# Decode block with adaptive layer norm: K/V rows of 24576 bytes in tiles of four heads, and a ring of four slots that also holds other weights

## The chip, the cores and the metric

The kernel runs on one core of a Trainium2 chip. The metric is the device time of one execution in microseconds (us): the median of several runs. A profile of one execution shows when each engine worked. TensorE (PE) does matrix products, VectorE (DVE) and ScalarE (ACT) work on tiles in SBUF and PSUM, GpSimd (POOL) fills constants, and SyncE (SP) issues nearly all transfers from HBM. SBUF has 128 partitions.

## The reference

One token per batch (B = 2) passes through attention over a cached window and a gated feed-forward network, both with a layer norm that is scaled and shifted by a condition `c`:

```python
mod = (silu(c) @ w_mod).reshape(2, 6, 1, 640)        # sa, ca, ga, sb, cb, gb
h = layernorm(x) * (1 + ca) + sa
q = (h @ wq)                                         # 32 heads of 192
k, v = last 1024 positions of the caches             # of 4096, per batch and head
o = softmax(q @ k.T * 192**-0.5) @ v
x = x + ga * (o.reshape(2, 1, 6144) @ wo)
h = layernorm(x) * (1 + cb) + sb
x = x + gb * ((gelu(h @ w_gate) * (h @ w_up)) @ w_down)
```

D is 640, F is 1536, all inputs are bf16. The two caches give 25.2 MB each (2 batches x 32 heads x 1024 keys x 192), w_mod 4.9 MB, wq and wo 7.9 MB each, and the three FFN weights 5.9 MB: 76.9 MB in all.

## The kernel before, in words

The program is a list of operations for each engine, written out by a small scheduler (`_Sched`, lines 28 to 101): `S.op` and `S.dma` append to an engine's list in the order of the Python code, and note which operations must have ended (reads and writes of named keys). Each engine runs its list in order; an operation that waits holds back all that stands behind it on that engine. Transfers from SP are one such list.

**Loads.** SP issues w_mod (38400 B per partition, line 297, into tile `r3`), then wq (61440 B per partition, line 298, into `r1`), and then the tiles of K and V into a ring of `NS` = 6 slots (`declare_ring`, lines 316 to 329). Afterwards it issues wo, into the memory of wq (lines 562 to 567), and w_gate, w_up and w_down in six pieces, into the memory of w_mod (568 to 582). These stand behind the last tile of V in SP's list.

**Tiles of K and V.** A tile holds two heads of both batches: 128 partitions are 32 groups `q` x 2 heads x 2 batches (`HB` = 4), and a partition has `J` = 32 keys of 192 numbers, 12288 B in a row of HBM. There are `NG` = 16 tiles of each kind. One transfer loads one batch's 64 partitions, so a tile is two transfers. The order is k0, k1, then k(g) and v(g-2) in turn. A slot is loaded again when the tile in it has been used.

**q.** `q_unit` (399 to 416) multiplies `hbm`, a tile that holds h spread over partitions, with a part of wq, so that each partition gets the q of its own head and batch: 10 matmuls of 384 columns for two tiles, then a copy to `qbc` by ScalarE. Two units run before the loop, and `filler` (418 to 429) runs the others inside the loop. Once they are all done, a filler is four matmuls of 512 columns whose result isn't used.

**The loop** (529 to 559) goes over tiles g, with later steps of the tiles before interleaved:

- `d_mul(g)`: VectorE multiplies the K tile by q (line 436).
- `p_reduce(g, part)`: TensorE adds up products over chunks of 16 numbers with an identity matrix, 12 matmuls of 512 columns (line 449); after the second half the K slot is free.
- `d_rows`, `p_maxT`, `d_max`: row sums, the partition maximum, a transpose, and the maximum of each head (458 to 473).
- `p_bias`, `d_bias`: two small matmuls spread the maximum and a large negative number for the partitions of other heads; VectorE adds it, ScalarE takes the exponent into `E_sb` with a column for every head and batch of the tile (476 to 489).
- `p_pv(g)`: TensorE multiplies E with V, 16 matmuls, four at a time in quarters of the array (line 499); then the V slot is free and ScalarE copies the result (506).
- `p_sel`, `d_norm`, `d_oT`: selection by constant matrices `SEL` and `DS`, division by the sum, and a transpose into `oT`, for two tiles together (509 to 527).

Steps of a tile stretch over four iterations. After the loop, five groups of matmuls multiply `oT` with wo (584 to 592), and the rest follows in order: `x1`, `layer_norm` (339 to 365), `ffn_gu` for gate and up, gelu, product, down, and the output by two transfers, one on SP and one on ScalarE's queue (636 and 637).

Ahead of the loop: POOL and VectorE build constants, `c` and `x` come by two transfers each on ScalarE's queue (lines 252 to 254), and `mod_part(0)`, the first layer norm and `mod_part(1)` follow when w_mod has landed.

Of the kernel before, what the change touches and what calls it, by code (L numbers as in the profile page):

```python
# [103 lines left out]
def bass_adaLN_cond__sliding_block_cached__geglu_ffn__decode_kernel(  # L104
# [23 lines left out]
    assert B == 2 and Dh == 192 and H % 4 == 0  # L128
# [6 lines left out]
    HB = 4  # L135
    QP = P // HB
    J = W // QP
    NQ = H * Dh
    NT = NQ // P
    NG = H // 2  # L140
    NGG = NG // 2
    ST = 4 * Dh // P
    SCALE = float(Dh) ** -0.5
    EPS = 1e-5
    GC = 512 // J
# [5 lines left out]
    NS = 6  # L151
    WO_SPLIT = [2, 2, 2, 1, 1]
    NWO = len(WO_SPLIT)
    assert sum(WO_SPLIT) == NGG
# [5 lines left out]
    QUP = 2  # L160
# [3 lines left out]
    with es:  # L164
# [6 lines left out]
        R3N = max(KT * 6 * D + KT * 2 * P, 2 * KT * F + FT * D)  # L171
        r3 = sb("r3", [P, R3N], BF16)
        wm_v = r3[:, 0:KT * 6 * D].rearrange("p (k n) -> p k n", k=KT)
        hbm_v = r3[:, KT * 6 * D:KT * 6 * D + KT * 2 * P].rearrange("p (k e m) -> p k e m", k=KT, e=2)
        wg_v = r3[:, 0:KT * F].rearrange("p (k n) -> p k n", k=KT)
        wu_v = r3[:, KT * F:2 * KT * F].rearrange("p (k n) -> p k n", k=KT)
        wd_v = r3[:, 2 * KT * F:2 * KT * F + FT * D].rearrange("p (f n) -> p f n", f=FT)
        qbc = sb("qbc", [P, NG, Dh], BF16)
        ring = sb("ring", [P, NS, J, Dh], BF16)
# [4 lines left out]
        P4 = sb("P4", [P, HB], F32)  # L184
        Bsel = sb("Bsel", [P, P], F32)
        SEL = sb("SEL", [P, 2, 2, P], BF16)
        DS = sb("DS", [P, 2, P], F32)
        par8 = sb("par8", [HB, P], F32)
        noff = sb("noff", [HB, HB], F32)
        zero_f = sb("zero_f", [HB, HB], F32)  # L190
# [15 lines left out]
        gmn = sb("gmn", [1, 2, HB], F32)  # L206
# [4 lines left out]
        rden = sb("rden", [P, 1], F32)  # L211
        oc = sb("oc", [P, Dh], BF16)
# [27 lines left out]
        sem_out = [S.sem("d_out%d" % i) for i in range(2)]  # L240
# [5 lines left out]
        def rows_of(tile, b):  # L246
            return tile[b:b + SQ * (NJ - 1) + 1:SQ, :]

        S.op("pool", lambda e: e.memset(cc[:, :], 0.0), writes=[("cc", 0), ("cc", 1)], name="cc0")
        S.op("pool", lambda e: e.memset(xc[:, :], 0.0), writes=[("xc", 0), ("xc", 1)], name="xc0")  # L250
        for b in range(2):
            S.dma("act", k_dma(rows_of(cc, b), c[b, :].rearrange("(j n) -> j n", j=NJ)), sem_c, writes=[("cc", b)], name="ld_c%d" % b)
        for b in range(2):
            S.dma("act", k_dma(rows_of(xc, b), A_x[b, 0, :].rearrange("(j n) -> j n", j=NJ)), sem_x, writes=[("xc", b)], name="ld_x%d" % b)
# [8 lines left out]
        S.op("pool", lambda e: e.affine_select(out=par8[:, :].rearrange("k (q c) -> k q c", c=HB),  # L263
                                               in_=ones_f[0:HB, :].rearrange("k (q c) -> k q c", c=HB),
                                               pattern=[[0, QP], [-1, HB]], compare_op=ALU.is_equal, fill=0.0,
                                               base=0, channel_multiplier=1),
             reads=["ones_f"], writes=["par8"], name="par8")
        S.op("pool", lambda e: e.affine_select(out=noff[:, :], in_=zero_f[:, :], pattern=[[-1, HB]],
                                               compare_op=ALU.is_equal, fill=BIG, base=0, channel_multiplier=1),
             reads=["zero_f"], writes=["noff"], name="noff")  # L270
        S.op("pool", lambda e: e.memset(SEL[:, :, :, :], 0.0), writes=["SEL"], name="SEL0")
        S.op("pool", lambda e: e.memset(DS[:, :, :], 1.0), writes=["DS"], name="DS1")
        hb0 = S.op("pool", lambda e: e.memset(hbm_v, 0.0), writes=["hbm"], name="hbm0")
# [3 lines left out]
        S.op("dve", lambda e: e.tensor_reduce(out=P4[:, :], in_=ident_f[:, :].rearrange("p (q c) -> p c q", c=HB), axis=AX.X, op=ALU.add),  # L277
             reads=["ident_f"], writes=["P4"], name="P4")
# [3 lines left out]

        for z in range(2):
            for jj in range(2):
                S.op("dve", (lambda z, jj: lambda e: e.tensor_copy(
                    out=SEL[:, z, jj, :].rearrange("p (a m) -> p a m", m=SQ)[:, 2 * z:2 * z + 2, 0:2],
                    in_=G32[:, HB * jj:HB * jj + HB].rearrange("p (h b) -> p h b", b=2)))(z, jj),
                    reads=["G32"], writes=["SEL"], name="SEL%d%d" % (z, jj))
            S.op("dve", (lambda z: lambda e: e.memset(DS[:, z, :].rearrange("p (a m) -> p a m", m=SQ)[:, :, 0:2], 0.0))(z),
                 writes=["DS"], name="DS0%d" % z)  # L290
            S.op("dve", (lambda z: lambda e: e.tensor_copy(
                out=DS[:, z, :].rearrange("p (a m) -> p a m", m=SQ)[:, 2 * z:2 * z + 2, 0:2],
                in_=P4[:, :].rearrange("p (h b) -> p h b", b=2)))(z),
                reads=["P4"], writes=["DS"], name="DS%d" % z)

        keep = {}
        keep["wm_dma"] = S.dma("sp", k_dma(r3[:, 0:KT * 6 * D], w_mod.rearrange("(p k) n -> p (k n)", k=KT)), sem_wm, writes=["wm"], name="ld_wm")
# [4 lines left out]
        for g in range(NG + 2):  # L302
            if g < NG:
                items.append(("k", g))
            if g >= 2:
                items.append(("v", g - 2))
# [6 lines left out]
        def ring_keys(slot):  # L313
            return [("ring", slot, b) for b in range(2)]

        def declare_ring(*consumed):
            ring_state["done"].update(place[it] for it in consumed)
            while ring_state["next"] < len(items) and (ring_state["next"] < NS or (ring_state["next"] - NS) in ring_state["done"]):
                s = ring_state["next"]
                kind, g = items[s]  # L320
                slot = s % NS
                cache = A_v_cache if kind == "v" else A_k_cache
                for b in range(2):
                    S.dma("sp", k_dma(ring[b:P:2, slot, :, :].rearrange("p j d -> p (j d)"),
                                      cache[b, 2 * g:2 * g + 2, K0:Sk, :].rearrange("h (q j) d -> q h (j d)", q=QP)),
                          sem_ring[slot], writes=[("ring", slot, b)], name="ld_%s%d_%d" % (kind, g, b))
                ring_state["next"] += 1

        declare_ring()


# [3 lines left out]
        S.op("act", lambda e: e.activation(out=sc[:, :], in_=cc[:, :], func=ACTF.Silu), reads=[("cc", 0), ("cc", 1)], writes=["sc"], name="silu")  # L335
        to_contraction(scT[:, :, :], sc[:, :], KT, ["sc"], ["scT"], "scT")
        S.op("dve", lambda e: e.tensor_copy(out=X2[:, 0, :], in_=xc[:, :]), reads=[("xc", 0), ("xc", 1)], writes=[("X2", 0)], name="x_f32")
# [30 lines left out]
        mod_pe = []  # L368

        def mod_part(part):  # L370
# [10 lines left out]
            mod_pe.append(S.op("pe", f, reads=["scT", "wm"], writes=[bank(bk)], name="mod%d" % part))  # L381
# [9 lines left out]
        for h in range(2):  # L391
            S.op("dve", (lambda h: lambda e: e.tensor_copy(
                out=hbm_v[:, :, h, :].rearrange("p k (q e b) -> p k q e b", e=2, b=2)[:, :, :, h, :],
                in_=hT[:, :, 0:2].unsqueeze(2).broadcast_to([P, KT, QP, 2])))(h),
                reads=["hT"], writes=["hbm"], name="hbm%d" % (h + 1))
# [3 lines left out]
        def q_unit():  # L399
# [4 lines left out]
            def f(e):  # L404
                last = None
                n = 0
                for h in range(2):
                    for k in range(KT):
                        last = e.matmul(ps[:, bk, 0:2 * Dh].rearrange("p (g d) -> p g d", g=2), lhsT=hbm_v[:, k, h, :],  # L409
                                        rhs=wq_v[:, k, 4 * u * Dh:4 * (u + 1) * Dh].rearrange("p (g e d) -> p g e d", g=2, e=2)[:, :, h, :],  # L410
                                        start=(n == 0), stop=(n == 2 * KT - 1))
                        n += 1
# [21 lines left out]
        def d_mul(g):  # L434
            ks = slot_of("k", g)
            S.op("dve", lambda e: e.tensor_tensor(out=ring[:, ks, :, :], in0=ring[:, ks, :, :],  # L436
                                                  in1=qbc[:, g, :].unsqueeze(1).broadcast_to([P, J, Dh]), op=ALU.mult),
                 reads=[("qbc", g // 2)], writes=ring_keys(ks), name="mul%d" % g)

        def p_reduce(g, part):  # L440
            ks = slot_of("k", g)
            bk = g % 2
            half = NCH // 2

            def f(e):
                last = None
                o_ap = ps[:, bk, 0:J * GC].rearrange("p (j c) -> p j c", j=J)
                for ci in range(part * half, (part + 1) * half):
                    last = e.matmul(o_ap, lhsT=ident_b[:, :], rhs=ring[:, ks, :, ci * GC:(ci + 1) * GC],  # L449
                                    start=(ci == 0), stop=(ci == NCH - 1))  # L450
                return last
            S.op("pe", f, reads=ring_keys(ks) + ["ident_b"], writes=[bank(bk)], name="red%d_%d" % (g, part))
# [238 lines left out]
```

## Time and profile before

| | us |
|---|---|
| median of 3 runs (190.31 to 190.89) | 190.63 |
| the profiled execution | 190.44 |
| its span (first to last instruction) | 188.7 |
| PE, DVE, ACT, POOL busy | 130.4, 91.6, 29.6, 3.8 |
| SP's DMA queue, share of 16 engines | 96.9% |
| w_mod landed, first use | 15.2 |
| wq landed, first use | 33.3 |
| last wo part, first use | 171.1 |
| last use of a w_down piece | 185.0 |

The page splits the span into 40 slices of 4.7 us; a digit is the busy share in tenths, and 9 is 90% or more. PEclk is the clock granted to TensorE in tenths of full speed. A row of a DMA queue gives packets, MB and the share of the time of 16 engines that its packets took; each row of a transfer (one partition's bytes) is one packet, and each transfer adds a 4-byte packet per engine that raises its semaphore. The chain of waits is followed back from the last instruction: each piece has its start, its duration and what it was. In a timeline a row gives the start, the duration, engine, line, operation, result and operands, and in brackets the idle time ahead of it and what ended it.

### The profile page before, as it was taken

Reading aid. Unit: us, or ns where it says so; the run is one execution under the profiler, and the core shown is the slowest. Engines: PE = TensorE matmul, PEld = TensorE weight load, DVE = VectorE, ACT = ScalarE, POOL = GpSimd, SP = SyncE. Lnnn points to the kernel's source line nnn. Section 1 sums busy time; section 2 is a strip of 40 time slices with the busy share of each in tenths; the row PEclk is TensorE's granted clock in tenths of the full one; section 3 lists DMA queues with packets and bytes.
Section 4 is the critical chain, followed back from the end, with each engine's and each line's share of the span. In section 5 each row is a group of like instructions: output and inputs, shape, how many; then the busy total and the mean of one; then the engine's idle time right before and its main releaser. Section 6 shows DMA issues by size and latency. Waiting matters only on the chain.

```text
span 188.7 us, 2624 instructions
## 1 busy us (share of the span) xinstructions
PE 130.4 (69%) x1091; PEld 65.0 (34%) x1100; DVE 91.6 (49%) x140; ACT 29.6 (16%) x75; POOL 3.8 (2%) x15
## 2 busy tenths in 40 slices
PE   0004500999999999999797798798887874353442
PEld 0001200455545445443343343344434443342211
DVE  7102600194756876964955856758648221003421
ACT  1003200121142121211110210120120223000400
POOL 8000000000000000000000000000000000000000
PEclk9999999999999999999999999999999995555555
DMA  7999997999999999999999999999999999999990
GB/s 252 399 509 482 430 430 302 425 430 423 432 422 425 428 421 425 425 423 427 427 427 419 427 427 425 419 425 427 425 427 423 417 418 422 417 430 425 414 369 13
DMA packets 7436, 77.04 MB, mean 408 GB/s; under 512 B 1281, under 2 KB 1281, under 8 KB 2817
## 3 DMA queue, kind: packets, MB, share of 16 engines
q1 hardware_dynamic: 7384, 76.88, 96.9%
q8 instruction: 8, 0.13, 0.3%
q14 instruction: 4, 0.02, 0.0%
q10 hardware_dynamic: 40, 0.01, 0.0%
HBM read 76.88 MB, written 0.00 MB: 407 GB/s over the span
## 4 chain that ended last, share of the span: by engine, by line
DMA 47%; PE 33%; SPq 14%; DVE 4%; issue 1%
DMA r<-in_A_wq_dram 17%; DMA ring<-in_A_k_cache_dram 16%; DMA r<-in_B_w_down_dram 14%; PE ps L449 14%; SPq L243 13%; PE ps L409 9%; PE ps L426 4%; DVE ring L436 4%; PE ps L499 2%; PE ps L479 1%; PE ps L514 1%; PE ps L480 1%; PE ps L626 1%; PE ps L466 1%; PE ps L516 0%
## 5 line engine op out<-in xcount | busy, mean ns | idle before, releaser
L436 DVE TENSOR_TENSOR ring<-ring,qbc 128x6144 bf16<-128x6144 bf16 x16 | 53.6, 3351 | 31.7 <-DMA ring<-in_A_k_cache_dram 17.6
L449 PE MATMUL ps<-ring,ident_b 128*128 128x512 bf16 x192 | 45.8, 380 | 7.7 <-DVE ring L436 7.7
L449 PEld LDWEIGHTS ps<-ring,ident_b 128*128 128x128 bf16 x192 | 18.0, 98 | 30.8 <-DVE ring L436 12.0
L426 PE MATMUL ps<-qbc,ident_b 128*128 128x512 bf16 x95 | 24.8, 379 | 1.0 <-issue 0.6
L409 PE MATMUL ps<-r 128*128 128x384 bf16 x80 | 16.7, 372 | 11.5 <-DMA r<-in_A_wq_dram 11.5
L409 PEld LDWEIGHTS ps<-r 128*128 128x128 bf16 x80 | 8.5, 109 | 19.7 <-issue 15.8
L506 ACT ACTIVATE On<-ps 128x384 bf16<-128x384 f32 x16 | 7.8, 490 | 46.7 <-PE ps L499 46.7
L377 PE MATMUL ps<-r,scT 128*32 128x480 bf16 x40 | 4.4, 600 | 15.2 <-DMA r<-in_w_mod_dram 15.2
L589 PE MATMUL ps<-r,oT 128*32 128x160 bf16 x192 | 7.3, 338 | 8.9 <-DMA r<-in_A_wo_dram 8.9
L499 PE MATMUL ps<-ring,E_sb 128*8 128x384 bf16 x256 | 13.2, 326 | 0.2 <-ACT E_sb L488 0.2
L426 PEld LDWEIGHTS ps<-qbc,ident_b 128*128 128x128 bf16 x104 | 9.2, 107 | 10.4 <-issue 4.3
L471 DVE TENSOR_REDUCE gmn<-ps 1x4 f32<-1x128 f32 x16 | 4.5, 279 | 15.2 <-PE ps L466 15.2
L458 DVE TENSOR_REDUCE S_sb<-ps 128x32 f32<-128x512 f32 x16 | 10.8, 677 | 0.0
L488 ACT ACTIVATE E_sb<-Sb_sb 128x128 bf16<-128x128 f32 x16 | 5.0, 309 | 34.8 <-DVE Sb_sb L485 34.8
L589 PEld LDWEIGHTS ps<-r,oT 128*32 128x32 bf16 x192 | 5.7, 141 | 10.3 <-DMA r<-in_A_wo_dram 10.3
L415 ACT ACTIVATE qbc<-ps 128x384 bf16<-128x384 f32 x8 | 3.9, 490 | 29.6 <-PE ps L409 29.6
L594 DVE TENSOR_TENSOR lnt<-ps,modC 128x160 f32<-128x160 f32 x1 | 0.3, 325 | 15.2 <-PE ps L589 15.2
L499 PEld LDWEIGHTS ps<-ring,E_sb 128*8 128x8 bf16 x256 | 4.8, 85 | 8.4 <-issue 5.5
L377 PEld LDWEIGHTS ps<-r,scT 128*32 128x32 bf16 x40 | 1.3, 132 | 16.5 <-issue 16.5
L485 DVE TENSOR_TENSOR Sb_sb<-S_sb,ps 128x128 f32<-128x128 f32 x16 | 4.5, 282 | 5.1 <-PE ps L480 5.0
L479 PEld LDWEIGHTS ps<-gmn,ones_f 1*128 1x128 f32 x32 | 4.7, 182 | 6.5 <-issue 5.8
L479 PE MATMUL ps<-gmn,ones_f 1*128 1x4 f32 x32 | 6.1, 258 | 0.0
(68 smaller groups left out, 86.4 us busy)
## 6 DMA issues: line engine op xcount, KB each, us to landing
ring<-in_A_k_cache_dram SPq DMA_DIRECT2D x32, 768.0 KB, 14.2
ring<-in_A_v_cache_dram SPq DMA_DIRECT2D x32, 768.0 KB, 16.2
r<-in_A_wq_dram SPq DMA_DIRECT2D x1, 7680.0 KB, 31.9
r<-in_A_wo_dram SPq DMA_DIRECT2D x3, 1920.0 KB, 25.7
r<-in_w_mod_dram SPq DMA_DIRECT2D x1, 4800.0 KB, 14.3
r<-in_A_wo_dram SPq DMA_DIRECT2D x2, 960.0 KB, 30.2
r<-in_B_w_gate_dram SPq DMA_DIRECT2D x1, 1920.0 KB, 30.0
r<-in_B_w_up_dram SPq DMA_DIRECT2D x1, 1152.0 KB, 30.0
```

Source lines behind the costliest of these rows:

```text
L243: return lambda e: e.dma_start(dst, src)
L377: last = e.matmul(ps[SQ * j:SQ * j + SQ, bk, 0:3 * DN].rearrange("p (i n) -> p i n", i=3), lhsT=scT[:, k, :], rhs=wm_v[:, k, 3 * part * D: ...
L409: last = e.matmul(ps[:, bk, 0:2 * Dh].rearrange("p (g d) -> p g d", g=2), lhsT=hbm_v[:, k, h, :], rhs=wq_v[:, k, 4 * u * Dh:4 * (u + 1) * ...
L426: last = e.matmul(ps[:, BK_Q[0], 0:512], lhsT=ident_b[:, :], rhs=qbc[:, 0:4, :].rearrange("p g d -> p (g d)")[:, 0:512], start=True, stop= ...
L436: S.op("dve", lambda e: e.tensor_tensor(out=ring[:, ks, :, :], in0=ring[:, ks, :, :], in1=qbc[:, g, :].unsqueeze(1).broadcast_to([P, J, Dh ...
L449: last = e.matmul(o_ap, lhsT=ident_b[:, :], rhs=ring[:, ks, :, ci * GC:(ci + 1) * GC], start=(ci == 0), stop=(ci == NCH - 1))
L458: S.op("dve", lambda e: e.tensor_reduce(out=S_sb[:, z, :], in_=ps[:, z, 0:J * GC].rearrange("p (j c) -> p j c", j=J), axis=AX.X, op=ALU.ad ...
L479: e.matmul(ps[:, BK_T, P:P + HB], lhsT=ones_f[0:1, :], rhs=gmn[:, z, :], start=True, stop=False)
L488: S.op("act", lambda e: e.activation(out=E_sb[:, z, :, :], in_=Sb_sb[:, z, :, :], func=ACTF.Exp, scale=SCALE, accum_out=esum[:, z:z + 1]), ...
L499: last = e.matmul(ps[r:r + 2 * HB, BK_O, 0:ON], lhsT=E_sb[:, z, 2 * jp:2 * jp + 2, :].rearrange("p j c -> p (j c)"), rhs=ring[:, vs, 2 * j ...
L506: S.op("act", lambda e: e.activation(out=On[:, z, :], in_=ps[:, BK_O, 0:ON], func=ACTF.Copy), reads=[bank(BK_O)], writes=[("On", z)], name ...
L589: last = e.matmul(ps[SQ * j:SQ * j + SQ, BK_M, 0:DN], lhsT=oT[:, t, :], rhs=wo_v[:, t, DN * j:DN * j + DN], start=(t == 0), stop=(t == NT ...
```

## The change

- A tile of K or V holds four heads (`HT` = 4): 128 partitions are 16 groups x 4 heads x 2 batches, a partition has 64 keys, and a row is 24576 B. There are 8 tiles of each kind; a tile is still two transfers.
- The ring has 4 slots of that size. Slots 2 and 3 first hold w_mod; `declare_ring(upto=2)` asks for k0 and k1 only, and the rest follows after the second product with w_mod. The order of tiles is k0, then k(g) and v(g-1) in turn. w_gate, w_up and w_down go into slots 0 and 1, and wait until v5's and k7's tiles have been used. `hbm` becomes a tile of its own.
- The multiply, the reduce, the row sums and the product with V work on halves of a tile (32 keys). All steps of a tile up to the exponent now stand in one iteration; the first half of its product with V is in the next iteration, the second half in the one after that. Before the loop there is one q unit of 20 matmuls, with four units in all.
- The two bias matmuls are one, with a constant row under the maximum. `E_sb` has 8 columns per key. `SEL` and `DS` have a second set for the second pair of heads.
- wo is read in rows of 15360 B: three whole parts of 12 tiles, and the fourth in parts of 8 and 4.
- `c`, `x` and the output are one transfer each, the output on SP's queue.

```diff
-    HB = 4
+    HB = 2 * HT
     QP = P // HB
     J = W // QP
+    JH = J // 2
-    NG = H // 2
+    NG = H // HT
-    NS = 6
-    WO_SPLIT = [2, 2, 2, 1, 1]
+    NS = 4
+    SL = J * Dh
+    WO_PARTS = [(0, 0, 12), (1, 0, 12), (2, 0, 12), (3, 0, 8), (3, 8, 4)]
-    QUP = 2
+    QUP = 1
...
+        hbm = sb("hbm", [P, KT, HT, P], BF16)
+        ring = sb("ring", [P, NS, J, Dh], BF16)
+        ring_f = ring[:, :, :, :].rearrange("p s j d -> p (s j d)")
+        wm_f = ring_f[:, 2 * SL:2 * SL + KT * 6 * D]
+        wg_v = ring_f[:, 0:KT * F].rearrange("p (k n) -> p k n", k=KT)
+        wu_v = ring_f[:, KT * F:2 * KT * F].rearrange("p (k n) -> p k n", k=KT)
+        wd_v = ring_f[:, 2 * KT * F:2 * KT * F + FT * D].rearrange("p (f n) -> p f n", f=FT)
...
+        S.dma("act", k_dma(rows_of(cc), dram_rows(c[:, :])), sem_c, writes=["cc"], name="ld_c")
+        S.dma("act", k_dma(rows_of(xc), dram_rows(A_x[:, 0, :])), sem_x, writes=["xc"], name="ld_x")
...
+        S.dma("sp", k_dma(wm_f, w_mod.rearrange("(p k) n -> p (k n)", k=KT)), sem_wm, writes=ring_keys(2) + ring_keys(3), name="ld_wm")
...
-        for g in range(NG + 2):
+        for g in range(NG + 1):
             if g < NG:
                 items.append(("k", g))
-            if g >= 2:
-                items.append(("v", g - 2))
+            if g >= 1:
+                items.append(("v", g - 1))
...
-                                      cache[b, 2 * g:2 * g + 2, K0:Sk, :].rearrange("h (q j) d -> q h (j d)", q=QP)),
+                                      cache[b, HT * g:HT * (g + 1), K0:Sk, :].rearrange("h (q j) d -> q h (j d)", q=QP)),
...
-        declare_ring()
+        declare_ring(upto=2)
...
         mod_part(0)
         layer_norm("ln1", 0, 0)
         mod_part(1)
+        declare_ring()
...
+        for g in range(NG + 2):
             has = g < NG
+            b1 = 1 <= g < NG + 1
+            b2 = g >= 2
+            done = b2 and g % 2 == 1
+            if has:
+                d_mul(g, 0)
             if b2:
+                p_pv(g - 2, 1)
             if has:
                 filler()
+                filler()
+                p_reduce(g, 0)
+                d_mul(g, 1)
+            if b2:
+                p_sel(g - 2)
+            if has:
+                filler()
+                p_reduce(g, 1)
+                d_rows(g, 0)
+            if done:
+                d_norm((g - 2) // 2)
+            if b1:
+                p_pv(g - 1, 0)
+            if has:
+                d_rows(g, 1)
+                d_part_max(g)
+                p_maxT(g)
+            if done:
+                d_oT((g - 2) // 2)
+            if has:
+                d_max(g)
+                p_bias(g)
+                d_bias(g)
+                filler()
...
+        r3_dead = [keep[("pv", NG - 3)], keep[("red", NG - 1)]]
...
-        for b, eng in enumerate(("sp", "act")):
-            S.dma(eng, k_dma(out[b, 0, :].rearrange("(j n) -> j n", j=NJ), rows_of(orow, b)), sem_out[b], reads=["orow"], name="st_out%d" % b)
+        S.dma("sp", k_dma(dram_rows(out[:, 0, :]), rows_of(orow)), sem_out, reads=["orow"], name="st_out")
```

## The prediction

> **What bounds the kernel now.** I read the busy table and the forty slices first, then the queue rows, the chain of waits, SP's waits, and last the timeline of TensorE at the three places where the stream of loads changes its row size.
>
> ```profile
> span 188.7 us, 2624 instructions
> PE 130.4 (69%) x1091; PEld 65.0 (34%) x1100; DVE 91.6 (49%) x140; ACT 29.6 (16%) x75; POOL 3.8 (2%) x15
> PEclk9999999999999999999999999999999995555555
> DMA  7999997999999999999999999999999999999990
> q1 hardware_dynamic: 7384, 76.88, 96.9%
> ```
> No compute engine is over 69%, but SP's queue keeps the 16 DMA engines busy for 96.9% of the span, from the second slice to the last but one. What loads take is the bound, and 76.9 MB is the same after the change. So only two things can move the time: what a byte costs in this stream, and a hole in the stream. The chain of waits ends the same way:
>
> ```profile
> 157.54 26.69 DMA r<-in_B_w_down_dram
> 184.23 0.04 issue
> 184.27 0.72 PE ps L626 x14
> ...
> 185.91 0.32 DVE orow L634
> ```
> The middle piece of w_down lands at 184.2 and the last near 185.0; the 3.7 us after that (the last products, two small steps on VectorE, the output) can't start earlier. The profiled execution is 190.44 us: 188.7 of span and 1.7 around it; the median of the runs is 190.63, so the execution that I sum against stands 0.2 us below it.
>
> What a byte costs depends on the row. These lines are TensorE's timeline (start, duration), an answer on the DMA queues for 45 to 145 us (only K/V rows there), and TensorE at wo:
>
> ```profile
> 15.18 2.19 PE L377 MATMUL ps<-r,scT 128*32 128x480 bf16 x20 [15.18 <-DMA r<-in_w_mod_dram]
> 33.29 7.95 PE L409 MATMUL ps<-r 128*128 128x384 bf16 x30 [11.51 <-DMA r<-in_A_wq_dram]
> ...
> DMA packets 4319, 42.48 MB, mean 425 GB/s; under 512 B 863, under 2 KB 863, under 8 KB 863
> ...
> 161.80 1.79 PE L589 MATMUL ps<-r,oT 128*32 128x160 bf16 x48 [2.89 <-DMA r<-in_A_wo_dram]
> 166.46 1.79 PE L589 MATMUL ps<-r,oT 128*32 128x160 bf16 x48 [2.87 <-DMA r<-in_A_wo_dram]
> ```
> w_mod is waited for until 15.18 and wq until 33.29: 7.864 MB of 61440 B rows in 18.11 us, 434 GB/s, or 2264 ns a row on each of 16 engines. K/V rows of 12288 B run at 425, 462.6 ns a row. A wo part of 16 rows per engine (7680 B) takes 166.46 - 161.80 = 4.66 us, 421 GB/s, 291 ns a row. A line through the two longer rows: (2264 - 462.6)/49152 = 0.03665 ns per byte, and 12.3 ns that a row costs whatever its size. It gives 293.8 for 7680 B, where 291 is measured, so the line holds to 1%.
>
> **The change, part by part.**
>
> K/V rows of 24576 B. Per DMA engine, 256 rows of 462.6 ns (118.4 us) become 128 of 12.3 + 24576 x 0.03665 = 913 ns (116.9 us): 1.56 us less. Bounds: nothing, if the rate of the 12288 B rows stays; the rate of the 61440 B rows would make it 50.33 MB/434 = 116.0 us, 2.4 less. I take the line, since 24576 lies between the two measured sizes. 64 transfers become 32; their closing writes are inside the 462.6.
>
> wo rows of 15360 B. Before 64 rows per engine by 291 = 18.6 us; after 24 of 575, 8 of 10240 B (388) and 8 of 5120 B (200) = 18.5. Gain 0.2 by the line for both (18.8 against 18.5: 0.3) or by the row (0.1); bounds 0 and 0.5 (434 GB/s throughout). The last wo part has 4 tiles where it had 6, 16 matmuls for 24, and lands last; from wo the chain of wo, layer norm, gate, up and down runs beside the FFN loads, so it only gets easier, and 0 is taken.
>
> The ring. Before, six slots are asked for at once and SP then waits 89.1 us in all for TensorE to free slots, with deep requests standing. After, v0 and k2 must wait in SP's queue until both w_mod products are done, because w_mod lies in slots 2 and 3. These ended at 21.8 us before; wq, k0 and k1 stand ahead until 33.3 + 2 x 7.3 = 47.9. Covered by 26 us. Behind that wait SP holds only later ring loads. The next slots are what needs care, since four slots are three loads of 7.3 us ahead of the one that is consumed:
>
> A q unit is now 20 matmuls instead of 10. By the first 30 (7.95 us, the first ten about 330 ns each) and the next 20 (3.25 us, 163 ns each), the first takes 33.3 to 39.6 and its copy ends at 40.1, before k0 lands at 40.6. VectorE multiplies k0 in two halves (3.35 us each by the same shape today) until 47.3. TensorE: two more q units until 46.1, twelve reduce matmuls (216 ns each, 2.6 us) until 48.7, the last q unit until 52.0, the second half until 54.6. That frees k0; v1 is asked for then, and the stream is filled until 33.3 + 4 x 7.3 = 62.5. Then comes the softmax part in the same iteration: row sums 0.68, maximum 0.2, transpose 0.27, 0.28, bias 0.31, bias add on 512 elements about 0.7 (an estimate from 282 ns at 128 and 557 ns for 384 elements out of PSUM) and hand-overs, until 57.4. k1's halves are multiplied until 64.1, reduced until 66.8; now k3 can be asked for, with about 1.0 us until data moves (w_mod: asked at 0.79; first packets about 1.8). The stream is filled until 62.5 + 7.3 = 69.8. So the tightest place has some 1.7 to 2 us to spare. Each later iteration takes 12 to 13 us (6.7 of multiplies, 2.6 of reduces, 2.5 to 3.5 of softmax) against 14.6 for a K and a V tile, so the slack grows by 1.5 to 2.5 us a tile. V slots are freed by the second half of the product at the start of the next but one iteration: v0 at about 70.5, wanted at 76. Cost 0; with that cover gone each us of lateness is one us of the end.
>
> Weights of the FFN in slots 0 and 1: w_gate waits for the products of v5 and k7's reduce, at about 146, and wo keeps the stream filled until 168. Only w_up and w_down are queued behind it. Free, where today the same loads wait for nothing. wo itself stands behind v7, which is asked for at about 133, 10 us before its turn.
>
> Set-up. hbm is 2560 elements per partition to clear (1.15 us for 1280 today, so 2.3) on POOL, which ends near 6 us and is read at 23; four copies of about 0.26 us for two, until 23.7, with wq at 33.3; a few more SEL and DS copies (0.17 to 0.48 us) on VectorE, idle until 11.7 but for 5.5 us. The loads of c and x become one each: the first product waits for w_mod at 15.18 and c is in at 11.3. All free. One bias matmul goes per tile, and selects, exponents and copies keep their totals within a few us: neither TensorE nor VectorE (about 10 of 14.6 us each) sets the end.
>
> The output. Two transfers by SP (0.66 us to issue) and ACT (0.59) become one by SP of twice the rows. SP waits 1.0 us, then 0.3. Bounds: 0.3 less, if ACT's half was the last; 0.6 more, if the second half costs a second issue. I take 0, since both halves were small and in parallel only in their issue.
>
> Sum: 190.44 - 1.56 - 0.2 = 188.7; 188.6 with the line used for wo too. I forecast 188.6, 2.0 below the median, by a ratio of 0.99. Its own range is 187.9 to 189.5 (the bounds of K/V and wo, less likely than the line, and output).
>
> A rule weighed: the Trainium skill (DMA: Bandwidth & Descriptors, section "Where 436 GB/s comes from") gives a ceiling of 435 GB/s for all 16 engines. The 434 of the 61440 B rows agrees with a ceiling there; by it alone K/V and wo could at best gain some 3.3 us, and the line stops short of it at 431.
>
> **The rivals.**
>
> *Ring runs dry (slower).* Place: the load of k3, whose slot comes free with k1's second reduce. The reckoning leaves 1.7 us. Against it: matmuls at 216 ns and multiplies at 3.35 us are measured. For it: everything from 33.3 to 66.8 is one chain, in which now all four q units stand ahead of k0's second half. If TensorE runs at half clock in that stretch (the first ten matmuls show it, and the clock row drops to 0.5 at 155), the 24 reduces of two halves and the fillers of an iteration cost 6 us more; 1.7 are covered, and an iteration of 19 us against 14.6 doesn't win it back. One such iteration gives 188.6 + 4.5 = 193; all of them would give over 210. It ends above today's from a hole of 2 us, lateness 3.7. The Trainium skill (TensorE: Matmul & The Clock Gate, section "Part 1: The HAM clock gate") puts the drop after an idle window of about 3.4 us. In the trace, steady gaps ahead of the reduces are 0.95 us with the clock at 1.0; after, I reckon 2.2 us (3.35 of multiply and the wait for the tile, less a V half and two fillers). By that rule the clock holds and this rival stays small. Chance 0.15.
>
> *Rows cost the same (no change).* The difference in rate could be that of wq's place in the stream, not of its rows: nothing else runs then, while K/V meets engines that read and write SBUF. Against it: wo at 421 with TensorE nearly idle is slower, as its shorter rows ask. Then 190.4. With a hole of 1 us on top of half the gain, 190.5 as well. Chance 0.14 with both forms.
>
> *More than the line* (434 GB/s for both, and ACT's half gone): 187.5. Chance 0.04.
>
> **How the numbers follow.** The forecast has 0.67. This kernel's runs spread by 0.6 us, so about 0.3% (0.57 us) is what can be told from no change. Faster (below 190.06): forecast, the rival above the line, and a little of the no-change case: 0.73. Same: 0.12, slower: 0.15. For eight in ten I take 187.9 to 190.9: it leaves out the dry ring (0.14) and the far gain (0.04).
>
> **What would show it.** K/V rows of 24576 B near 913 ns, 431 GB/s in mid-stream; the DMA row at 9 from the second slice on, with no lower digit at 65 to 75 us; v7 ending near 150, wo near 168.7, w_down near 182.4; SP waiting for TensorE ahead of every ring load. Wrong would be a hole in the DMA row near 69 us, TensorE below clock 1.0 before 150, or a rate that stays at 425.

## The result and the profile after

The changed kernel takes 297.88 us (295.36 to 304.48, six runs) where the kernel before takes 190.61: a ratio of 1.559, with a 95% interval of 1.553 to 1.566. Two of its six runs (300.99 and 304.48) were slow ones, and the ratio leaves them out. The forecast was 188.6, with a range of 187.9 to 190.9. The profiled execution is 297.68 us, 295.6 of it span.

The page of the changed kernel, the busy table, the granted clock, the DMA rows and the queue:

```profile
span 295.6 us, 2398 instructions
PE 145.4 (49%) x1056; PEld 66.0 (22%) x1056; DVE 93.4 (32%) x115; ACT 23.8 (8%) x47; POOL 5.6 (2%) x16
PEclk9999998799985796589759765995698579655555
DMA  8999999999999999999999999999999999999993
GB/s 333 466 399 399 296 239 218 216 226 213 213 215 216 236 223 214 226 218 233 223 223 219 213 238 223 226 219 236 226 225 219 243 229 239 216 418 422 423 417 123
q1 hardware_dynamic: 4444, 76.88, 97.9%
```

VectorE's work is nearly unchanged (91.6 before, 93.4 now); TensorE's 145.4 where it had 130.4 come at a lower granted clock (0.779 on average, 0.912 before). The DMA row is at 9 as before, and the queue is busy for 97.9% of a span that is 107 us longer: the same 76.88 MB, in fewer packets, keep the 16 DMA engines busy for longer. There is no hole in it. The GB/s row shows where: from slice 6 to slice 35 the rate is 213 to 243, and these are the K/V rows; ahead of them and behind them it is what it was. An answer on the DMA queues for 60 to 130 us, when only K/V rows move:

```profile
DMA packets 793, 15.53 MB, mean 222 GB/s; under 512 B 160, under 2 KB 160, under 8 KB 160
```

The small packets are those that raise semaphores, so 633 rows of 24576 B moved in 70 us on 16 engines: 70 x 16/633 = 1.77 us a row. The forecast was 913 ns, and the kernel before took 463 ns for half the bytes. Per engine, 128 rows of 1.77 us in place of 256 of 0.463 are 226.6 - 118.5 = 108 us: the whole loss.

The chain of waits in the changed kernel shows what follows from it:

```profile
74.32 0.54 SPq L248
74.90 45.48 DMA ring<-in_A_k_cache_dram
120.41 3.37 DVE ring L453
...
129.89 2.60 PE ps L464 x12
132.56 0.54 SPq L248
133.14 43.42 DMA ring<-in_A_k_cache_dram
```

Each tile of K is asked for as soon as its slot is free and lands some 45 us later, behind three other tiles of 14 to 15 us each. TensorE is idle for half of that, and its granted clock falls in between (5 to 8 in the clock row where it was 9); a slower TensorE costs nothing here, since the requests stand long before their turn.

So the question is not where a wait is, but why a K/V row costs twice what it should.

### The profile page after: what moved, and what is told of

It reads as the page before. It is cut to its first block, busy times and chain, and to the rows that moved or that the text cites. A ratio compares the mean times of both kernels' runs of the same rounds, so it can differ in the third digit from the quotient of the medians.

```text
span 295.6 us, 2398 instructions
## 1 busy us (share of the span) xinstructions
PE 145.4 (49%) x1056; PEld 66.0 (22%) x1056; DVE 93.4 (32%) x115; ACT 23.8 (8%) x47; POOL 5.6 (2%) x16
## 3 DMA queue, kind: packets, MB, share of 16 engines
q1 hardware_dynamic: 4444, 76.88, 97.9%
HBM read 76.88 MB, written 0.00 MB: 260 GB/s over the span
## 4 chain that ended last, share of the span: by engine, by line
DMA 69%; PE 15%; SPq 7%; DVE 7%; issue 0%; DVEq 0%
DMA ring<-in_A_k_cache_dram 60%; PE ps L464 12%; DMA ring<-in_B_w_down_dram 10%; SPq L248 7%; DVE ring L453 6%; PE ps L443 1%; PE ps L426 1%; PE ps L536 0%; PE ps L532 0%; DVE S_sb L473 0%; DVE Sb_sb L500 0%; PE ps L654 0%; PE ps L495 0%; DVE fin L660 0%; DVE orow L662 0%
## 5 line engine op out<-in xcount | busy, mean ns | idle before, releaser
L464 PE MATMUL ps<-ring,ident_b 128*128 128x512 bf16 x192 | 58.8, 471 | 78.1 <-DVE ring L453 78.1
L443 PE MATMUL ps<-qbc,ident_b 128*128 128x512 bf16 x116 | 29.5, 389 | 0.0
L515 PE MATMUL ps<-ring,E_sb 128*16 128x384 bf16 x256 | 14.9, 363 | 20.8 <-DMA ring<-in_A_v_cache_dram 20.8
L426 PE MATMUL ps<-r,hbm 128*128 128x384 bf16 x80 | 15.8, 365 | 12.1 <-DMA r<-in_A_wq_dram 12.1
L503 ACT ACTIVATE E_sb<-Sb_sb 128x512 bf16<-128x512 f32 x8 | 5.0, 630 | 117.1 <-DVE Sb_sb L500 117.1
L426 PEld LDWEIGHTS ps<-r,hbm 128*128 128x128 bf16 x80 | 8.6, 108 | 19.9 <-issue 15.9
L515 PEld LDWEIGHTS ps<-ring,E_sb 128*16 128x16 bf16 x256 | 5.4, 94 | 30.6 <-DMA ring<-in_A_v_cache_dram 20.9
L393 PE MATMUL ps<-ring,scT 128*32 128x480 bf16 x40 | 4.4, 600 | 14.8 <-DMA ring<-in_w_mod_dram 14.8
L500 DVE TENSOR_TENSOR Sb_sb<-S_sb,ps 128x512 f32<-128x512 f32 x8 | 5.5, 689 | 3.9 <-PE ps L495 3.9
L532 PE MATMUL ps<-On,SEL 128*128 128x192 bf16 x32 | 4.4, 267 | 1.2 <-ACT On L523 1.2
```

What stands on the lines that cost most here:

```text
L393: last = e.matmul(ps[SQ * j:SQ * j + SQ, bk, 0:3 * DN].rearrange("p (i n) -> p i n", i=3), lhsT=scT[:, k, :], rhs=wm_v[:, k, 3 * part * D: ...
L443: last = e.matmul(ps[:, BK_Q[0], 0:512], lhsT=ident_b[:, :], rhs=qbc[:, 0:4, :].rearrange("p g d -> p (g d)")[:, 0:512], start=True, stop= ...
L464: last = e.matmul(o_ap, lhsT=ident_b[:, :], rhs=ring[:, ks, hf * JH:(hf + 1) * JH, ci * GC:(ci + 1) * GC], start=(ci == 0), stop=(ci == NC ...
L500: S.op("dve", lambda e: e.tensor_tensor(out=Sb_sb[:, z, :, :], in0=S_sb[:, z, :].unsqueeze(2).broadcast_to([P, J, HB]), in1=ps[:, BK_T, P: ...
L503: S.op("act", lambda e: e.activation(out=E_sb[:, z, :, :], in_=Sb_sb[:, z, :, :], func=ACTF.Exp, scale=SCALE, accum_out=esum[:, z:z + 1]), ...
L515: last = e.matmul(ps[r:r + 2 * HB, BK_O, 0:ON], lhsT=E_sb[:, z, 2 * jp:2 * jp + 2, :].rearrange("p j c -> p (j c)"), rhs=ring[:, vs, 2 * j ...
```

## The experiments

I held three theories. A: reads from HBM or the way that they are dealt are at fault, since a transfer now reads 16 groups of four heads, 1.5 MiB apart, where it read 32 groups of two. B: writes into every other partition collide when rows are long. C: a row of 24576 B as such is slow. In all that follows, rows are counted from an answer on the DMA queues for 60 to 130 us, as above; the figures for a row in the expectations differ from these by up to 2%. Each kernel of the experiments ran once, but for the last one; the differences that the argument rests on are 20 us and more.

### One thing of the load at a time

The first four runs change only the K/V loads of the changed kernel. Source from one whole head:

```diff
-cache[b, HT * g:HT * (g + 1), K0:Sk, :].rearrange("h (q j) d -> q h (j d)", q=QP)
+cache[b, HT * g, :, :].rearrange("(q j) d -> q (j d)", j=J)
```

> The K/V loads take one whole head (4096 keys, one unbroken 1.5 MiB of HBM) for each transfer of 64 rows of 24576 B, in place of 16 groups of the last 1024 keys of four heads; destination, row size, bytes and all other work stay, and the attention is of other keys. The changed kernel shows 1758 ns a K/V row where the line gave 913. Theory A (reads collide, since the four heads lie 1.5 MiB apart and 16 groups x 4 heads are dealt to the 16 engines): the rows fall to about 913 ns and the time to 188 to 190 us. Theory B (writes collide: long rows into every other partition): 1758 ns and 295 to 300 us stay. Theory C (a row of 24576 B as such is slow): the same as B.

Source of 32 groups of two heads, with the long rows:

```diff
-cache[b, HT * g:HT * (g + 1), K0:Sk, :].rearrange("h (q j) d -> q h (j d)", q=QP)
+cache[b, HT * g:HT * g + 2, Sk // 2:Sk, :].rearrange("h (q j) d -> q h (j d)", q=2 * QP)
```

> The K/V loads take 32 groups of two heads, as the kernel before does, but with rows of 24576 B (the last 2048 keys of two heads); destination, row size and all other work stay, and the attention is of other keys. Theory A in the form that the deal of 16 groups x 4 heads is at fault: about 913 ns a row and 188 to 190 us. Theory B or C: 1758 ns and 295 to 300 us stay. If the heads' distance of 1.5 MiB is at fault at any number of heads, something in between.

Destination in blocks of neighbouring partitions:

```diff
-ring[b:P:2, slot, :, :]
+ring[b * (P // 2):(b + 1) * (P // 2), slot, :, :]
```

> The K/V loads write each batch into 64 neighbouring partitions (0 to 63, 64 to 127) in place of every other partition; source, row size and all other work stay, and each partition's keys are of another head or batch than its q. Theory B (writes collide: long rows into every other partition): the rows fall to about 913 ns and the time to 188 to 190 us. Theory A or C: 1758 ns and 295 to 300 us stay.

Rows of half the length:

```diff
-for b in range(2):
-    S.dma("sp", k_dma(ring[b:P:2, slot, :, :] ...
+for hf in range(2):
+    for b in range(2):
+        S.dma("sp", k_dma(ring[b:P:2, slot, hf * JH:(hf + 1) * JH, :] ...
...
-    sem_ring[slot]
+    sem_ring[2 * slot + hf]
```

> Each K/V transfer is split into two, of the first and the last 32 keys of each partition, so rows are 12288 B again, in the same layout (16 groups x 4 heads into every other partition); the halves have their own semaphores. The result stays the same as the reference's. Theory A (the deal of groups and heads, or the distance of the heads): twice the 12288 B row of 463 ns, so about 880 ns, and 290 to 300 us. Theory B or C (row size, with or without the stride of partitions): 463 ns a row, 425 GB/s, and 189.5 to 191 us.

Measured, beside 190.35 us for the kernel before: one head 190.47, two heads 189.84, blocks 307.63, halves 276.03. In the order one head, two heads, blocks, halves (each line is that answer for one of these kernels):

```profile
DMA packets 1524, 29.97 MB, mean 428 GB/s; under 512 B 303, under 2 KB 303, under 8 KB 303
```
```profile
DMA packets 1525, 29.97 MB, mean 428 GB/s; under 512 B 304, under 2 KB 304, under 8 KB 304
```
```profile
DMA packets 768, 14.92 MB, mean 213 GB/s; under 512 B 160, under 2 KB 160, under 8 KB 160
```
```profile
DMA packets 1718, 16.93 MB, mean 242 GB/s; under 512 B 341, under 2 KB 341, under 8 KB 341
```

A row of 24576 B takes 917 ns in the first two (1221 rows in 70 us), near the forecast 913, and 1.84 us in the third. Rows of 12288 B in the fourth take 813 ns where the kernel before has 463. So C falls: long rows go at full rate with another source, and short rows are slow with this one too. B in its first form falls too: the first two write every other partition. What is at fault comes with the source of 16 groups of four heads. The halves were better than I had expected for that case (813 against 880 ns).

### The source, or where the engines write

Two causes were left. A1: the four heads' distance of 1.5 MiB in HBM. A2: with 16 groups outermost each DMA engine gets one group, and so the 16 engines write at any time into partitions that share half of the paths into SBUF. The next three runs hold one fixed and move the other. The same bytes as in the run with one head, but dealt as 16 groups:

```diff
-cache[b, HT * g, :, :].rearrange("(q j) d -> q (j d)", j=J)
+cache[b, HT * g, :, :].rearrange("(h q j) d -> q h (j d)", h=HT, q=QP)
```

> The same bytes as in the run with one whole head per transfer (which took 919 ns a row), the same destination and row size, but read as 4 blocks of 16 groups, with the groups outermost, as the changed kernel reads its four heads; the blocks lie 384 KiB apart, not 1.5 MiB. The attention is of other keys. Theory A1 (the heads' distance of 1.5 MiB in HBM): 919 ns and 190 us stay. Theory A2 (the deal: with 16 outermost groups each DMA engine gets one group, so the 16 engines write at any time into 16 partitions 8 apart, which share half of the paths into SBUF): about 1760 to 1815 ns, 217 to 225 GB/s, 290 to 300 us.

The source of one head, into neighbouring partitions:

```diff
 cache[b, HT * g, :, :].rearrange("(q j) d -> q (j d)", j=J)
-ring[b:P:2, slot, :, :]
+ring[b * (P // 2):(b + 1) * (P // 2), slot, :, :]
```

> The same source as in the run with one whole head per transfer (919 ns a row), but each batch goes to 64 neighbouring partitions instead of every other one. The attention is of other keys. Theory A1 or any cause in HBM: the source is the fast one, so 919 ns and 190 us. Theory A2, with paths into SBUF that belong to groups of partitions: 64 neighbours are only half of them, so about 1815 ns and 217 GB/s however the rows are dealt, 298 to 308 us.

The source of the changed kernel, 16 rows at a time into 16 neighbouring partitions:

```diff
-for b in range(2):
-    S.dma("sp", k_dma(ring[b:P:2, slot, :, :] ...
+for h in range(HT):
+    for b in range(2):
+        c0 = QP * (2 * h + b)
+        S.dma("sp", k_dma(ring[c0:c0 + QP, slot, :, :].rearrange("p j d -> p (j d)"),
+                          cache[b, HT * g + h, K0:Sk, :].rearrange("(q j) d -> q (j d)", q=QP)),
```

> The source is that of the changed kernel, but each head and batch is a transfer of its own: 16 rows of 24576 B, one per DMA engine, into 16 neighbouring partitions; eight transfers a tile. Each partition's keys are of another head or batch than its q. Theory A1 or any cause in HBM: the reads at any time are those of the changed kernel, so 1700 to 1800 ns and about 298 us. Theory A2: 16 neighbouring partitions are a quarter of the paths (4 of 16, if 4 neighbours share one, which the half rate at a distance of 8 suggests), so a row takes about 3630 ns, K/V run at some 108 GB/s, and the time is about 298 + 233 = 530 us.

And the kernel before with the deal alone:

```diff
-cache[b, 2 * g:2 * g + 2, K0:Sk, :].rearrange("h (q j) d -> q h (j d)", q=QP)
+cache[b, 4 * (g // 2):4 * (g // 2) + 4, K0 + (g % 2) * (W // 2):K0 + (g % 2 + 1) * (W // 2), :].rearrange("h (q j) d -> q h (j d)", q=QP // 2)
```

> The kernel before with one part of the change alone: its K/V transfers, still of 12288 B rows into every other partition, read 16 groups of four heads (half of the window) instead of 32 groups of two heads. The attention is of other keys. If the deal over the engines is the cause: rows near the 797 ns that halved rows of the changed kernel took, about 240 GB/s, so 275 to 280 us with nothing else of the change. If something else in the changed kernel is needed for it (row size, ring, w_mod in it): 463 ns and 190.4 us.

Measured, beside 190.65 us for the kernel before: 296.82, 309.57, 451.48 and 279.60. The same answer for the four, in this order:

```profile
DMA packets 788, 15.48 MB, mean 221 GB/s; under 512 B 157, under 2 KB 157, under 8 KB 157
```
```profile
DMA packets 768, 14.92 MB, mean 213 GB/s; under 512 B 160, under 2 KB 160, under 8 KB 160
```
```profile
DMA packets 735, 9.04 MB, mean 129 GB/s; under 512 B 367, under 2 KB 367, under 8 KB 367
```
```profile
DMA packets 1711, 16.84 MB, mean 241 GB/s; under 512 B 341, under 2 KB 341, under 8 KB 341
```

- The first reads the bytes of the one-head run, into the same partitions, without four heads 1.5 MiB apart, and is as slow as the changed kernel (1.77 us a row). A1 falls; how the rows are dealt is enough.
- The second has the source of the one-head run, and differs from it only in the destination: 213 GB/s, half of 428. So here the limit is on the side of SBUF: 64 neighbouring partitions take half of what every other partition takes.
- The third has the changed kernel's source and an even narrower destination: 368 rows in 70 us, 3.04 us a row. It moves as A2 says and as no cause in HBM would (nor do eight transfers a tile explain it: their 4-byte packets, one to a row, took 35 ns in the median), but less than expected: a quarter of the paths in step would have been 3.63 us and 530 us. Transfers follow each other without a wait, and an engine that is done goes on into the next 16 partitions, so the engines do not all stand on the same quarter; that reason is argued, not measured.
- The fourth puts the deal alone into the kernel before: 818 ns for a row of 463, and 89 us more. Nothing else of the change is needed for the loss.

One rival is left by these four: the deal also changes which rows are read at the same time. The second and the third run show that the destination alone can set the rate, but no run keeps the reads of the changed kernel as they are and only spreads its writes.

### In step, or not

If engines share paths two by two, half rate needs both of a pair in the same place at the same time. Within a transfer an engine's four rows go to partitions 8e, 8e+2, 8e+4 and 8e+6 (plus the batch), so in A2 it spends two rows on one group of four partitions and two on the next. If engine e + 4 is two rows behind, the pair should never meet. Small extra transfers ahead of the K/V stream make such a delay:

```diff
+for n, c0s in ((12, (0, 2)), (4, (4, 6))):
+    for c0 in c0s:
+        phase.append(S.dma("sp", k_dma(ring[c0:c0 + 9 * (n - 1) + 1:9, 1, :, :].rearrange("p j d -> p (j d)"),
+                                       A_k_cache[0, 0, 0:n * J, :].rearrange("(q j) d -> q (j d)", q=n)), sem_ph, ...))
...
+deps=phase if slot == 1 else ()
```

> The changed kernel with four small extra transfers ahead of k0: two of 12 rows of 24576 B and two of 4 rows, into slot 1 before k1 is asked for (k1 waits for them). They are meant to give DMA engines 0 to 3 four rows, 4 to 7 and 8 to 11 two rows and 12 to 15 none ahead of the K/V stream, if transfers of 12 and 4 rows use the lowest engines; so engines e and e+4, which I take to share a path into SBUF, are two rows apart. Result as the reference's. Theory A2 with engines in step (two rows into even groups of four partitions, then two into odd ones, e and e+4 always in the same): the shift takes them apart, rows fall to 910 to 1200 ns, 330 to 427 GB/s, and the time to 193 to 220 us, 3.65 us of it the extra rows. If sharing is not by phase but by the deal as such: about 1758 ns and 300 us.

The second kernel has twice as many of them (`c0` 0, 2, 4, 6 for 12 rows and 1, 3, 5, 7 for 4 rows).

> The same with twice as many extra transfers, so that the engines are four rows apart, which is a whole period of the four rows of a transfer. Theory A2 with engines in step: back in step, about 1750 ns, 223 GB/s and 300 to 306 us. If any delay between engines were enough: as with two rows.

Measured, beside 190.55: 260.38 with two rows, 301.42 with four. With two rows the page (GB/s in 40 slices of 6.5 us) and the answers for 45 to 76 us and 80 to 100 us are:

```profile
GB/s 285 470 463 447 363 244 360 354 365 365 369 396 247 242 236 237 244 246 244 263 259 293 276 270 297 293 323 320 311 293 320 256 224 214 408 429 414 334 60 13
```
```profile
DMA packets 582, 11.53 MB, mean 372 GB/s; under 512 B 113, under 2 KB 113, under 8 KB 113
```
```profile
DMA packets 238, 4.65 MB, mean 232 GB/s; under 512 B 48, under 2 KB 48, under 8 KB 48
```

With four rows, the answer for 60 to 130 us is:

```profile
DMA packets 837, 16.49 MB, mean 236 GB/s; under 512 B 165, under 2 KB 165, under 8 KB 165
```

So the four-row delay wins little (236 GB/s, where the changed kernel has 222) and pays for its extra rows. With two rows, the same loads of the same kernel run at 372 GB/s (469 rows in 31 us, 1.06 us a row) and then at 232. In between, SP's timeline shows:

```profile
63.91 1.17 SPq L248 DMA_DIRECT2D ring<-in_A_v_cache_dram  x2
76.24 1.19 SPq L248 DMA_DIRECT2D ring<-in_A_k_cache_dram  x2
```

The request for k3 comes at 76.24, too late for the faster stream. It doesn't stop as a whole: by the packets' times in the trace, thirteen of the 16 engines still move rows from 76.5 to 77.7 us, and three have none: a small hole.

Each engine ends its share of a transfer with a 4-byte packet, so the times of these packets tell which engines keep step. In the changed kernel 16 of them come from 73.9 to 76.6 us, none until 80.9, and 16 again from 81.2 to 83.8. With two rows of delay they come in eights (8 from 71.5 to 73, 8 from 73.5 to 75.5). After that hole they come as eleven (84.3 to 87) and five (87.7 to 89.2). Later they spread out, and the rate rises (323 and 320 GB/s in slices 27 and 28). With four rows of delay twelve come together and four apart from them (71.8 to 74.2, 75.2 to 76.8).

So the rate goes with the step: 372 GB/s for eight and eight, 232 for eleven and five, 236 for twelve and four, 222 for all 16 together. That is what A2 in step asks for in kind, but not in size. If engines shared paths by fixed pairs alone, at least one of the five, an odd number, would have had its partner among the eleven and kept its rate; yet no row that starts from 80 to 100 us takes less than 1.3 us, where 457 of 469 did from 45 to 76. Which engines share what stays open, and so does whether the order of the reads has a part in it. My number missed, since I had counted no hole in that stream.

### What the rest of the change is worth

The variant with 32 groups of two heads is the changed kernel without its fault. It was timed, beside 190.55 for the kernel before:

> The run with 32 groups of two heads and rows of 24576 B again, timed: all of the change but the deal (the attention is of other keys). By the prediction's sum the change without its fault should give 188.6 to 188.8; the single look gave 189.84 against 190.35. If the difference to the prediction is chance, 188.6 to 189.2; if it is real (engines that end further apart, small holes near 68 to 74 us), 189.5 to 190.0, a ratio of 0.994 to 0.998.

It took 190.02 us (188.96 to 190.69, ten runs), a ratio of 0.9967 with an interval of 0.9947 to 0.9987. That is faster by 0.1 to 0.5%, less than the 1% that I had summed. Its profiled execution is 189.18, 187.1 of it span:

```profile
q1 hardware_dynamic: 4444, 76.88, 96.6%
```

96.6% of 187.1 is 180.7 us of packets, where 96.9% of 188.7 is 182.8. So the stream did become 2.1 us lighter; 1.3 us arrive in this execution, 0.5 in the median. TensorE's waits in the tail show the part that does (start, duration, and the wait in brackets):

```profile
156.05 1.01 PE L617 MATMUL ps<-r,oT 128*32 128x160 bf16 x48 [0.47 <-DMA r<-in_A_wo_dram]
...
183.03 1.22 PE L654 MATMUL ps<-ring,aT 128*32 128x160 bf16 x24 [0.42 <-DMA ring<-in_B_w_down_dram]
```

The first wo part is waited for until 156.05, against 157.13 before, and w_down until 183.03, against 184.27:

```profile
157.13 1.79 PE L589 MATMUL ps<-r,oT 128*32 128x160 bf16 x48 [1.27 <-DMA r<-in_A_wo_dram]
```

What takes back the rest is known in part. The run with 32 groups of two heads above is the same kernel, at 189.84 us. For 64 to 78 us its answer and, below it, that of the timed execution are:

```profile
DMA packets 299, 5.79 MB, mean 414 GB/s; under 512 B 63, under 2 KB 63, under 8 KB 63
DMA packets 307, 5.96 MB, mean 426 GB/s; under 512 B 64, under 2 KB 64, under 8 KB 64
```

SP asked for k3 at 66.40 there, and at 65.49 in the timed one. The lower rate is worth some 0.4 us (an estimate: 14 us x (1 - 414/426)), of 0.66 between the two executions. The rest isn't settled: the spread from run to run is 1.7 us, against 0.3 for the kernel before.

No version here beats the kernel before and computes the same. The layout of four heads with 64 keys always has 16 groups per head, and the variants at full rate read other keys.

## Why the prediction was wrong

The step that failed is the first of the sum, "K/V rows of 24576 B". It took the price of a row from a line through two row sizes, and its bounds from the same two rates: nothing gained, or the rate of the 61440 B rows. All those rows were moved in transfers of another shape than the new one: wq into 128 partitions, K/V in 32 groups of two heads. The change alters the size and the deal together, and I priced the size alone. The line itself holds: with the old deal a row of 24576 B took 917 ns against 913. With the new one it took 1.77 us, which adds 108 us where the step said 1.56 less.

The bounds were wrong for the same reason. For a resource that the trace did not show (transfers dealt in another shape) I excluded a loss without giving a reason for it. "Rows cost the same" was the worst that I allowed for the rows. (The step's own bounds, with those of wo and of the output, sum to 187.2 and 191.0, wider than the 187.9 to 189.5 that I gave, and the far gain is 187.2, not 187.5; 297.88 lies far outside all of them.)

The rival on the other side, the ring that runs dry, did not happen in the changed kernel: the DMA row is 9 from the second slice to the last but one. Its times were good all the same. In the timed variant with the old deal, SP asked for v1 and k3 at

```profile
53.16 1.18 SPq L248 DMA_DIRECT2D ring<-in_A_v_cache_dram  x2
65.49 1.18 SPq L248 DMA_DIRECT2D ring<-in_A_k_cache_dram  x2
```

where I had 54.6 and 66.8. The spare of 1.7 to 2 us was not as good: in the execution where SP asked at 66.40, the packets' times show up to four of the 16 engines without a row between 68 and 69 us. I had taken the engines to end together, at 69.8. So the four slots nearly keep up at full rate, and where I put cost 0 it was some 0.4 us in that execution, by the estimate above.

The clock was said to hold, at gaps of 2.2 us. In the timed variant it does until about 159; in the changed kernel TensorE waits up to 12.9 us for the product of a tile and the clock falls (0.67 on average from 110 to 121 us). The rule on idle windows in the Trainium skill (TensorE: Matmul & The Clock Gate, section "Part 1: The HAM clock gate") agrees with that. It is an effect there, not the cause.

wo: in the changed kernel two parts are waited for until 268.37 and 272.96, so a part of 8 rows per engine takes 4.59 us, 574 ns a row; the forecast was 575. The single output transfer: SP waits 1.0 us for it, as before, and its extra 0.3 is gone. That bound of the step was the right one. In the timed variant the last 4.10 us after 183.03 were 4.40 after 184.27. Set-up, w_mod in the ring and the wait for FFN weights cost nothing, as said: v0 is asked for at 21.5 us, far ahead of its turn, and wo runs straight behind the last V tile.

Two sections of the Trainium skill bear on what the runs show. DMA: Bandwidth & Descriptors (section "Why a DMA increments its semaphore by 16 and not by 1") has the number of engines follow from the outermost dimension of both sides, and 16 groups still give 16 engines, as the traces agree: all of them were busy. SBUF — State Buffer (section "Door 1: The DMA port swizzle (why `[64,N]` ≈ `[32,N]`)") says that four neighbours share a port, that partitions 32 apart share it too, and those 64 apart do not. By that, 64 neighbours have 8 of 16 ports (213 of 428 GB/s here), and partitions 8e for sixteen engines hit only 8 at a time (222 here); both agree. That the groups are given out one per engine, while 32 groups or a flat run of 64 rows are given out in another way, is my inference from which loads ran at full rate: no trace here names the engine of a packet. The map of ports could have raised the question beforehand, since the new source has 16 outermost groups of four rows; I looked at the row's length alone.

## What to carry to other kernels

A transfer's price is not its bytes and row size alone: when a change reshapes a load, ask which partitions the DMA engines write at the same time, and keep the shape of a load that is known to be fast. A DMA row at 9 says that engines are busy, not that they move at full rate; read GB/s beside it. When a forecast rests on one price times hundreds of rows, bound that price on the side of a loss too, unless a run with the same shape excludes it.

## What the runs showed of the hardware

- With rows of 24576 B, the same bytes into the same partitions move at 428 GB/s as a flat run of 64 rows and at 221 as 16 groups of four rows.
- 64 neighbouring partitions take 213 GB/s, every other partition up to 428. 16 neighbours, one transfer after another, take 129.
- The loss depends on how many engines are in step: 222 GB/s with all 16, 236 with twelve, 232 with eleven, and 372 with two groups of eight that are two rows apart.
- Shorter rows lose a little less with the slow deal: 241 and 242 GB/s at 12288 B, 221 and 222 at 24576.
